# Loading the second dense block of x from GpSimd's queue, and zeroing two x buffers later

## The chip, the cores and the metric

The kernel runs on one core of a Trainium2 chip. A core has TensorE (PE, with its weight loads as PEld), VectorE (DVE), ScalarE (ACT), GpSimd (POOL) and SyncE (SP), which work each through a list of its own and wait for one another on semaphores; transfers run on 16 DMA engines that all queues share. The metric is the device time of one execution in microseconds (us), taken as the median of several.

## What is computed

A causal depthwise convolution over seven tokens, with softmax weights per head, is followed by a feed-forward layer whose hidden value is the largest of three products. Inputs and outputs are float32.

```python
# x: 8 x 4160 x 192, weight: 8 heads x 7, w1, w2, w3: 192 x 768, w_out: 768 x 192
w = softmax(weight)                                     # per head, over the 7 taps
y[b, s, h, :] = sum_k w[h, k] * x_padded[b, s + k, h, :]  # six zero rows ahead of each sequence
y = y.reshape(33280, 192)
h = maximum(maximum(y @ w1, y @ w2), y @ w3)            # 33280 x 768
out = h @ w_out                                         # 33280 x 192
```

The kernel writes the maximum as w3's product plus a maximum of the differences: it keeps `wd` = w1 - w3, w2 - w3 in fp16, takes `max(relu(y @ (w1 - w3)), y @ (w2 - w3))` as the hidden value, and adds `y @ (w3 @ w_out)` through a small matrix `m`.

## The kernel before, in words

The 33280 tokens are cut into 65 blocks of 512 tokens. Blocks 0 to 3 are "dense": their convolution reads x in pieces of 112 rows (`xf`, float32, five pieces to a block), cast to two zero-padded fp16 tiles `xz[t][0]` and `xz[t][1]`. Blocks from 4 on take another road: x is loaded as rows of 39 partitions at two places of an `xf` buffer (partitions 0 to 38 and 64 to 102), GpSimd casts partitions 0 to 102 in one instruction (L199), and since partitions 39 to 63 hold no rows there, partitions 32 to 63 of such a buffer are zeroed once (`zero_x`, L140 on ACT, L137 elsewhere) before its first load of this kind. There are seven `xf` buffers; blocks 4, 5 and 6 use buffers 4, 5 and 6 for the first time and then share them in turn.

The order on each engine is written out by hand. The list of SP's queue at the start is: x0 (two transfers, L167), the first third of the weights (columns 0 to 255) as three transfers of 128 rows (L229) and three of 64 rows (L233), x1 (one transfer of 112 x 5 pieces of 768 bytes, 420 KB, L167), the second third by L229, the other two thirds of the 64-row parts by L233, the last third by L229, w_out (`wos`, L248), x2, x3, and, once their buffers are zeroed, x4, x5, x6.

While these come in, the start of the compute lists is:

- DVE zeroes tiles, casts x0 to `xz[0]` (L216), copies a part of the convolution's band (L297), makes the differences `wd` (L312), zeroes one half of buffer 6 (L137), casts one half of block 0's convolution (L393), moves the lower rows of w3 up by 64 partitions (L316), makes one more difference.
- ACT zeroes buffer 4 (L140), copies its part of the band, zeroes all of buffer 5 (L140), casts the other half of block 0's convolution (L393), zeroes the other half of buffer 6 (L140), casts its share of x1 (L216).
- POOL makes an identity matrix, waits for x1, casts its share of it to `xz[1]` (L216), then casts w3 (L320), moves the rest of w3 up (L316), makes four differences (L312), casts again, copies across (L323), casts w_out to `wo` (L713) and casts x2 and x3 to `xz` (L216).
- PE keeps itself warm, makes the band (L293), does the convolution of block 0 (L388, output D), the first products of block 0 that need only `wd` columns 0 to 255 and one half of the convolution (L541, part "F"), the convolution of block 1 (L388), the other products of blocks 0 and 1 in turn (L541), transposes w3 (L338), multiplies the hidden values of block 0 by `wo` (L613), does the convolution of block 2 (L388), makes `m` (L347), and from block 2 on runs a steady loop: products of one block (L517) between the output products of the block before (L582) and convolutions of later blocks (L367).

Of the kernel before, what the change touches and what calls it, by code (L numbers as in the profile page):

```python
# [15 lines left out]
P = 128  # L16
# [7 lines left out]
HALF = P // 2  # L24
# [4 lines left out]
def kernel(  # L29
# [12 lines left out]
    nc = tc.nc  # L42
    ctx.enter_context(tc.manual_schedule())

    B, SEQ, D = x.shape
# [12 lines left out]
    for b in range(B):  # L58
        s = nfull * NBLK
        while s < SEQ:  # L60
            n = min(SEQ - s, NBLK - off)
# [28 lines left out]
    NR = NBLK // TOK // 2  # L90
# [3 lines left out]
    def rows_of(t):  # L94
        rows = [(b, S + o) for (b, S, N, off) in blocks[t] for o in range(0, N, TOK)]
        assert len(rows) == 2 * NR
        return rows
# [23 lines left out]
    def get_x(t):  # L121

        if not 0 <= t < NB or t in xin:
            return
        if t < XBUF:
            xbuf.append(const.tile([P, NR, D], FP32, name=f"xf_{t}"))
        xf = xbuf[t % XBUF if t < NDENSE + XBUF else NDENSE + (t - NDENSE - XBUF) % 3]
        assert all(v[0] is not xf for v in xin.values())
        xin[t] = [xf, 0, ()]

    def zero_x(t, q0=0, q1=NR, eng=None):

        if t >= NDENSE:
            get_x(t)
        xf = xbuf[t]
        if eng is not None:
            eng.memset(xf[TOK:HALF, q0:q1, :], 0.0)  # L137
            return
        zero = idle[TOK:HALF, 0:D]
        nc.scalar.copy(out=xf[TOK:HALF, q0:q1, :],  # L140
                       in_=bass.AP(tensor=zero.tensor, offset=zero.offset,
                                   ap=[list(zero.ap[0]), [0, q1 - q0], [1, D]]))

    def load_x(t, eng=nc.sync):
        if not 0 <= t < NB:
            return
        loaded.add(t)
        get_x(t)
        xf = xin[t][0]
        if t < NDENSE:  # L150
            todo = [(0, c[3], c[1] * SEQ + c[2], i) for i, c in enumerate(chunks_of[t])]
        else:
            todo = [(HALF * (i // NR) + (0 if s else LAP), KR if s else TOK,
                     b * SEQ + s - (LAP if s else 0), i % NR) for i, (b, s) in enumerate(rows_of(t))]
        parts = []
        i, n = 0, len(todo)
        row = [c[2] for c in todo]
        while i < n:
            k = i
            while k + 1 < n and todo[k + 1][:2] == todo[i][:2] and row[k + 1] - row[k] == row[i + 1] - row[i]:  # L160
                k += 1
            step = row[i + 1] - row[i] if k > i else 0
            p0, rlen, _, q0 = todo[i]
            q1 = todo[k][3] + 1
            src = bass.AP(tensor=x.tensor, offset=row[i] * D,
                          ap=[[D, rlen], [step * D, q1 - q0], [1, D]])
            eng.dma_start(out=xf[p0:p0 + rlen, q0:q1, :], in_=src)  # L167
            if parts and parts[-1][0] == rlen:
                parts[-1] = (rlen, parts[-1][1], q1)
            else:  # L170
                parts.append((rlen, q0, q1))
            i = k + 1
        xin[t] = [xf, todo[0][0], parts]
# [33 lines left out]
    def cast_dense(t, copies, slots_=range(CYC // 32)):  # L207
        xf, _, parts = xin.pop(t)
        for v, copy in enumerate(copies):
            if copy is None:  # L210
                continue
            for s in slots_:
                cut = GRP * (32 * s // GRP + 1)
                a, b = (32 * s, cut) if v == 0 else (cut, 32 * s + 32)
                for (rl, q0, q1) in parts:
                    copy(  # L216
                        out=xz[t][v][0:rl, q0:q1, :].rearrange("p q (k c) -> p q k c", c=CYC)[:, :, :, a:b],
                        in_=xf[0:rl, q0:q1, :].rearrange("p q (k c) -> p q k c", c=CYC)[:, :, :, a:b])
# [8 lines left out]
    def load_wa(f):  # L227
        for st, n, wsrc in ((w3s, 0, moe_w3), (ws, 0, moe_w1), (ws, 1, moe_w2)):
            nc.sync.dma_start(out=st[:, n, f], in_=wsrc[0:P, f])  # L229

    def load_wb(f):
        for st, lo, n, wsrc in ((w3s, 0, 1, moe_w3), (ws, 0, 2, moe_w1), (ws, HALF, 2, moe_w2)):
            nc.sync.dma_start(out=st[lo:lo + HALF, n, f], in_=wsrc[P:D, f])  # L233

    wk = const.tile([NHEAD, SMALL], FP32, name="wk")[:, 0:KW]
    nc.scalar.dma_start(out=wk[:], in_=weight)
# [4 lines left out]
    load_x(0)  # L241
    load_wa(slice(0, PW))
    load_wb(slice(0, PW))
    load_x(1)
    load_wa(slice(PW, 2 * PW))
    load_wb(slice(PW, DFF))
    load_wa(slice(2 * PW, DFF))
    nc.sync.dma_start(out=wos[:], in_=moe_w_out.rearrange("(j p) c -> p j c", p=P))  # L248
# [3 lines left out]
    make_identity(nc, ident[:])  # L252
    ident16 = const.tile([P, P], FP16)
    nc.gpsimd.tensor_copy(out=ident16[:], in_=ident[:])
    idle = const.tile([P, NBLK], FP16)
    nc.vector.memset(idle[:], 0.0)
    def keep_warm(widths, pool, tag):

        ps = pool.tile([P, NBLK], FP32, tag=tag, name="idle")
        for n in widths:  # L260
            nc.tensor.matmul(ps[:, 0:n], lhsT=idle[:, 0:P], rhs=idle[:, 0:n], start=True, stop=True)
# [27 lines left out]
    for lo, hi, copy in ((0, CUT, nc.scalar.copy), (CUT, WIN, nc.vector.tensor_copy)):  # L289
# [6 lines left out]
        for a in range(4):  # L296
            copy(out=band[32 * a:32 * a + 32, :, 32 * a + lo:32 * a + hi],  # L297
                 in_=bps[:, 0:hi - lo, :].rearrange("p c h -> p h c"))
    zero_x(5)
    keep_warm((NBLK,) * 3, psp, "p")  # L300


# [7 lines left out]
    def make_wd(n, j0, j1, eng=nc.vector):  # L310
        f = slice(P * j0, P * j1)
        eng.tensor_sub(out=wd[:, n, f], in0=ws[:, n, f], in1=w3s[:, n // 2, f])  # L312

    def copy_w3(copy, j0, j1):
        f = slice(P * j0, P * j1)
        copy(out=w3s[HALF:P, 1, f], in_=w3s[0:HALF, 1, f])  # L316

    def cast_w3(j0, j1):
        f = slice(P * j0, P * j1)
        nc.gpsimd.tensor_copy(out=w3h[:, :, f], in_=w3s[:, :, f])  # L320
# [8 lines left out]
    def w_of(i, c, j):  # L329
        n = side(i, c)  # L330
        n = i if n == 0 else NC if n == 1 else 2
        return wd[HALF * i:HALF * (i + 1), n, P * j:P * (j + 1)]
# [110 lines left out]
    def y_all(t, i, c):  # L443
        if t < NDENSE:
            return dense[t][HALF * i:HALF * (i + 1), side(i, c), :]
        a = y_row(t, i)
        s0, s1, s2, s3 = (spot(t, i, c, r) for r in range(4))
        assert s3 - s2 == s1 - s0
        return bass.AP(tensor=a.tensor, offset=a.offset + P * s0,
                       ap=[list(a.ap[0]), [P * (s2 - s0), 2], [P * (s1 - s0), 2], [1, P]])  # L450
# [39 lines left out]
    def meet():  # L490

        emit(True)
        assert not ops
        clock[0] = clock[1] = 0
# [32 lines left out]
    def l1_dense(tiles, parts="FH"):  # L527

        meet()
        for part in parts:  # L530
            order = [(i, v) for i in range(2) for v in tiles] if part == "F" else [(i, v) for v in tiles for i in range(2)]
            for i, (t, j, pools) in order:
                pool, tag = pools[i]
                if (t, j, i) not in open_ps:
                    open_ps[t, j, i] = pool.tile([P, NBLK], FP32, tag=tag, name=f"l{tag}{i}_{t}_{j}")
                    begun.discard((t, j, i))
                if part == "F":
                    a, b = wd[:, i, P * j:P * (j + 1)], dense[t][:, 0, :]
                else:
                    a, b = w_of(i, NC - 1, j), y_all(t, i, NC - 1)  # L540
                nc.tensor.matmul(open_ps[t, j, i][:], lhsT=a, rhs=b,  # L541
                                 start=(t, j, i) not in begun, stop=(t, j, i) in begun)
                begun.add((t, j, i))
# [143 lines left out]
    PQ = ((psp, "p"), (psq, "q"))  # L687
    WW = ((psw, "w"), (psw, "w"))
    WPWQ = ((psw, "w"), (psp, "p"), (psw, "w"), (psq, "q"))
    ACT, DVE = nc.scalar.copy, nc.vector.tensor_copy  # L690
    GP = nc.gpsimd.tensor_copy
    make_wd(0, 0, 2)
    make_wd(1, 0, 2)
    zero_x(6, 4, NR, nc.vector)
    conv_dense(0, (ACT, DVE))
    zero_x(6, 0, 4)
    for t in range(NDENSE, XBUF):
        load_x(t)
    copy_w3(DVE, 0, 2)
    make_wd(2, 0, 2)  # L700
    cast_dense(1, (GP, ACT), (1, 2, 0))
    l1_dense([(0, 0, PQ), (0, 1, PQ)], "F")
    cast_w3(0, 2)
    copy_w3(GP, 2, 6)
    make_wd(2, 2, 4, nc.gpsimd)
# [144 lines left out]
```

## Time and profile before

| what | us |
|---|---|
| median of three runs (lowest, highest) | 452.57 (452.45, 454.37) |
| the profiled execution, its own time | 453.55 |
| its span, first to last instruction | 451.8 |
| PE busy in the span | 445.6 |
| ACT, DVE, POOL busy | 320.4, 356.3, 203.7 |
| granted TensorE clock, mean | 1.000 |
| PE's share of the chain that ended last | 95% |

The span is shorter than the execution's time by 1.75 us, which lies before the first and behind the last instruction. A profile shows one execution; it gives when each instruction ran, what an engine waited for, and in time order the chain of work that ended last. PE is busy for nearly the whole span, so what is left to gain or lose lies where PE is not busy: 7.50 us of the first 10 us are, 9.78 of the next ten, 9.46 of the ten behind those, and 9.97 of those from 30 to 40.

### The profile page before, as it was taken

What the parts mean: (1) busy time and instruction counts of PE and PEld (TensorE: products, weight loads), DVE (VectorE), ACT (ScalarE), POOL (GpSimd) and SP (SyncE); (2) the same over time, 40 slices, a digit from 0 to 9 for tenths busy, and PEclk for the clock granted to TensorE, in tenths of its full rate; (3) what the DMA queues carried; (4) which work ended last, traced back from release to release, by engine and by line L of the source; (5) the groups of instructions that cost most, each with busy time, mean ns of one, the idle gap of its engine ahead of it and who ended that gap; (6) DMA issues with size and microseconds to landing.
All of it is one profiled execution on the core that took longest, in us unless ns stands there. A gap on an engine that the chain in (4) does not pass through costs nothing.

```text
span 451.8 us, 18261 instructions
## 1 busy us (share of the span) xinstructions
PE 445.6 (99%) x7576; PEld 409.5 (91%) x7576; DVE 356.3 (79%) x610; ACT 320.4 (71%) x600; POOL 203.7 (45%) x234
## 2 busy tenths in 40 slices
PE   7999999999999999999999999999999999999997
PEld 4479999999999999999999999999999999999996
DVE  7768778878878787787787887887887887887775
ACT  7867777767777676676776776776776776776664
POOL 2784826556455524724824625526533544224000
DMA  6979999595875659649559749659549677142123
GB/s 201 247 178 160 199 186 209 152 222 160 181 210 149 174 124 210 164 117 204 162 130 196 182 111 199 180 99 227 158 113 197 171 158 143 54 136 75 58 71 106
DMA packets 128242, 72.01 MB, mean 159 GB/s; under 512 B 52320, under 2 KB 127967, under 8 KB 128159
## 3 DMA queue, kind: packets, MB, share of 16 engines
q1 hardware_dynamic: 127999, 70.75, 68.3%
q8 instruction: 59, 0.97, 1.1%
q14 instruction: 24, 0.20, 0.2%
q10 hardware_dynamic: 160, 0.10, 0.1%
HBM read 33.28 MB, written 25.56 MB: 130 GB/s over the span
## 4 chain that ended last, share of the span: by engine, by line
PE 95%; SPq 2%; DMA 2%; POOL 0%; issue 0%; DVE 0%; POOLq 0%
PE po L582 36%; PE lq L517 32%; PE lp L517 22%; PE G L367 3%; DMA wos<-in_moe_w_out_dram 2%; SPq L229 1%; SPq L233 1%; PE po L613 0%; PE D L388 0%; PE po L640 0%; SPq L167 0%; POOL wo L713 0%; PE pm L347 0%; PE po L657 0%; PE po L621 0%
## 5 line engine op out<-in xcount | busy, mean ns | idle before, releaser
L582 PE MATMUL po<-wo,h 64*128 64x192 f16 x3024 | 331.7, 243 | 0.0
L505 DVE TENSOR_TENSOR h<-r,lq 128x512 f16<-128x512 f16 x384 | 262.8, 685 | 84.9 <-ACT r L500 74.9
L500 ACT ACTIVATE r<-lp 128x512 f16<-128x512 f32 x384 | 228.9, 597 | 113.7 <-PE lp L517 102.8
L517 PE MATMUL lp<-yp,wd 64*128 64x512 f16 x1098 | 295.6, 376 | 0.0
L517 PE MATMUL lq<-yp,wd 64*128 64x512 f16 x1098 | 295.5, 376 | 0.0
L582 PEld LDWEIGHTS <-h 64*128 64x128 f16 x3024 | 242.7, 94 | 5.3 <-issue 4.1
L517 PEld LDWEIGHTS <-wd 64*128 64x128 f16 x2268 | 181.7, 94 | 14.8 <-issue 0.2
L199 POOL CAST x<-xf 103x768 f16<-103x768 f32 x122 | 97.1, 824 | 113.8 <-DMA xf<-in_x_dram 109.2
L582 PE MATMUL po<-m,yp 64*128 64x192 f16 x720 | 140.3, 243 | 0.0
L430 POOL COPY yp<-yp 64x1536 f16<-64x1536 f16 (+1 forms) x70 | 90.9, 1298 | 85.1 <-DMA yp<-ys 42.0
L590 DVE TENSOR_TENSOR o<-a,po 128x384 f32<-128x384 f32 x126 | 69.0, 547 | 0.0
L582 PEld LDWEIGHTS <-yp 64*128 64x128 f16 x720 | 66.3, 94 | 0.1
L589 ACT COPY a<-po 128x384 f32<-128x384 f32 x126 | 59.6, 473 | 0.0
L407 ACT CAST ys<-G 128x480 f16<-128x480 f32 (+1 forms) x53 | 25.4, 530 | 9.5 <-PE G L367 9.5
L407 DVE CAST ys<-G 128x480 f16<-128x480 f32 (+1 forms) x53 | 30.1, 610 | 0.0
L367 PE MATMUL G<-x,band 39*32 39x240 f16 (+3 forms) x1024 | 16.5, 242 | 0.0
L367 PEld LDWEIGHTS <-band 39*32 39x32 f16 x1024 | 10.2, 92 | 4.6 <-issue 4.5
L517 PE MATMUL lq<-yd,wd 64*128 64x512 f16 x36 | 9.7, 376 | 0.0
L517 PE MATMUL lp<-yd,wd 64*128 64x512 f16 x36 | 9.7, 376 | 0.0
L541 PEld LDWEIGHTS <-wd 128*128 128x128 f16 (+1 forms) x48 | 3.1, 96 | 6.1 <-issue 2.7
L216 POOL CAST xz<-xf 112x160 f16<-112x160 f32 (+2 forms) x15 | 4.2, 323 | 8.4 <-DMA xf<-in_x_dram 8.3
L388 PEld LDWEIGHTS <-xz 112*32 112x32 f16 x320 | 4.1, 100 | 2.6 <-POOL xz L216 1.1
(79 smaller groups left out, 98.7 us busy)
## 6 DMA issues: line engine op xcount, KB each, us to landing
xf<-in_x_dram SPq DMA_DIRECT2D x113, 234.0 KB
out_dram<-o SPq DMA_DIRECT2D x62, 384.0 KB
wall<-in_moe_w_dram SPq DMA_DIRECT2D x12, 128.0 KB
xf<-in_x_dram SPq DMA_DIRECT2D x7, 204.8 KB
xf<-in_x_dram SPq DMA_DIRECT2D x3, 420.0 KB
yp<-ys SPq DMA_TRANSPOSE x70
out_dram<-o SPq DMA_DIRECT2D x5, 192.0 KB
wos<-in_moe_w_out_dram SPq DMA_DIRECT2D x1, 576.0 KB
```

The lines of the kernel that those rows point to most:

```text
L199: nc.gpsimd.tensor_copy(out=x16s[t0][0:K, :, :, u, r, :].rearrange("p h j c -> p j h c"), in_=xf[0:K, 4 * r:4 * r + 4, :].rearrange("p j ( ...
L229: nc.sync.dma_start(out=st[:, n, f], in_=wsrc[0:P, f])
L233: nc.sync.dma_start(out=st[lo:lo + HALF, n, f], in_=wsrc[P:D, f])
L367: nc.tensor.matmul(G[2 * (k // per) + i][TOK * j:TOK * (j + 1), k % per, :], lhsT=band[row, h, HALF * i + LAP:HALF * i + KR], rhs=x16s[t0] ...
L407: copy(out=slots[t][:, i % 2, :, :, GRP * h0:GRP * (h0 + per)].rearrange("p u r (h c) -> p h (u r) c", c=GRP), in_=G[i][:].rearrange("p h ...
L430: nc.gpsimd.tensor_copy(out=yp[HALF * i:HALF * (i + 1), 1, :, :, :, :].rearrange("p i u k n -> p (i u k n)"), in_=yp[HALF * (1 - i):HALF * ...
L500: nc.scalar.activation(out=r[:], in_=ps[0][:], func=AF.Relu)
L505: nc.vector.tensor_max(out=hs[t][:, j, :], in0=r[:], in1=q[:])
L517: nc.tensor.matmul(ps[i][:], lhsT=w_of(i, c, j), rhs=y_all(t, i, c), start=(n == 0), stop=(n == NC - 1))
L582: nc.tensor.matmul(ps[b0, i][:, s % 2, :], lhsT=a, rhs=b, start=first, stop=last)
L589: nc.scalar.copy(out=a[:], in_=ps[s - 1, 0][:])
L590: nc.vector.tensor_add(out=outs[t][:, s - 1:s + 1, :], in0=a[:], in1=ps[s - 1, 1][:])
```

## The change

x1 is no longer in SP's queue: the buffer is only reserved there, and the load is issued by GpSimd, right behind its copy of the identity matrix. Everything behind x1 on SP's queue moves up by one place. The move of the first third of w3's lower rows (`copy_w3(…, 0, 2)`) goes from DVE to GpSimd, ahead of GpSimd's share of x1's casts. Buffer 5 is zeroed half by ACT, half by DVE, behind the casts of block 0's convolution and of x1, instead of all by ACT ahead of them. Buffer 6 is zeroed all by GpSimd, behind its share of x1's casts, instead of half by DVE and half by ACT. `load_wb` gets a parameter that keeps its old value in every call.

```diff
-    def load_wb(f):
+    def load_wb(f, eng=nc.sync):
         for st, lo, n, wsrc in ((w3s, 0, 1, moe_w3), (ws, 0, 2, moe_w1), (ws, HALF, 2, moe_w2)):
-            nc.sync.dma_start(out=st[lo:lo + HALF, n, f], in_=wsrc[P:D, f])
+            eng.dma_start(out=st[lo:lo + HALF, n, f], in_=wsrc[P:D, f])
@@
     load_x(0)
     load_wa(slice(0, PW))
     load_wb(slice(0, PW))
-    load_x(1)
+    get_x(1)
     load_wa(slice(PW, 2 * PW))
@@
     nc.gpsimd.tensor_copy(out=ident16[:], in_=ident[:])
+    load_x(1, nc.gpsimd)
     idle = const.tile([P, NBLK], FP16)
@@
-    zero_x(5)
+    get_x(5)
     keep_warm((NBLK,) * 3, psp, "p")
@@
     make_wd(0, 0, 2)
     make_wd(1, 0, 2)
-    zero_x(6, 4, NR, nc.vector)
+    copy_w3(GP, 0, 2)
     conv_dense(0, (ACT, DVE))
-    zero_x(6, 0, 4)
+    make_wd(2, 0, 2)
+    cast_dense(1, (GP, ACT), (1, 2, 0))
+    zero_x(5, 0, 4)
+    zero_x(5, 4, NR, nc.vector)
+    l1_dense([(0, 0, PQ), (0, 1, PQ)], "F")
+    zero_x(6, eng=nc.gpsimd)
     for t in range(NDENSE, XBUF):
         load_x(t)
-    copy_w3(DVE, 0, 2)
-    make_wd(2, 0, 2)
-    cast_dense(1, (GP, ACT), (1, 2, 0))
-    l1_dense([(0, 0, PQ), (0, 1, PQ)], "F")
     cast_w3(0, 2)
     copy_w3(GP, 2, 6)
```

## The prediction

> **What bounds the kernel now.** I read the page's busy times first, then the chain that ended last, in order of time, then PE's own waits, and last the timeline and the transfers of the first microseconds, where the change is. The busy times, and the waits of PE over the whole span (us in total, times, longest):
>
> ```profile
> PE 445.6 (99%) x7576; PEld 409.5 (91%) x7576; DVE 356.3 (79%) x610; ACT 320.4 (71%) x600; POOL 203.7 (45%) x234
> ...
> PE lp L541 <- ACT yd L393: 0.7, 1, 0.7
> PE D L388 <- POOL xz L216: 0.6, 1, 0.6
> PE po L613 <- POOL wo L713: 0.5, 1, 0.5
> PE lq L541 <- DVE h L505: 0.2, 1, 0.2
> ```
>
> PE bounds all but the start. Asked for the waits of PE behind 25 us, the trace lists none. So whatever moves PE's entry into its steady loop moves the end by as much, and nothing else that the change touches can. The four waits are all that the start can give, beside a start of the whole chain that is earlier. That chain (start, us, what):
>
> ```profile
> 5.05 0.59 SPq L167
> ...
> 8.98 1.42 SPq L229
> ...
> 11.40 7.90 DMA wos<-in_moe_w_out_dram
> 19.42 1.15 POOL wo L713
> 20.61 2.14 PE po L613 x24
> 22.75 1.04 PE D L388 x76
> ```
>
> SP's queue sends the loads one behind the other; the nineteenth transfer on it, w_out, lands at 19.30; POOL casts it; PE waits 0.54 us for the cast. The timeline shows the other gate, x1 (start, us, instructions, idle time before them and what ended it):
>
> ```profile
> 6.11 1.48 ACT L140 CAST xf<-idle 32x1536 f32<-32x1536 f16 x1
> 7.61 0.58 ACT L393 CAST yd<-D 128x512 f16<-128x512 f32 x1
> 8.24 0.59 PE L541 MATMUL lp<-yd,wd 128*128 128x512 f16 x2 [0.65 <-ACT yd L393]
> 9.45 0.91 POOL L216 CAST xz<-xf 112x160 f16<-112x160 f32 x3 [7.79 <-DMA xf<-in_x_dram]
> 9.88 1.30 PE L388 MATMUL D<-band,xz 112*32 112x103 f16 x80 [0.61 <-POOL xz L216]
> 21.06 3.39 POOL L216 CAST xz<-xf 112x240 f16<-112x240 f32 x12 [0.50 <-DMA xf<-in_x_dram]
> ```
>
> x1 is issued at 5.05 and its readers start at 9.40 (ACT) and 9.45 (POOL): 4.35 us. And ACT's zeroing of buffer 5 stands in front of the cast that PE waits for at 8.24. The transfers from 0 to 16 us, in slices of 0.4 us:
>
> ```profile
> GB/s 0 0 0 0 29 188 334 349 295 159 141 328 287 156 174 113 58 100 338 361 373 308 336 305 353 205 195 159 228 256 215 247 224 161 276 326 321 315 326 325
> ```
>
> From 5.2 to 7.2 us the engines moved 156, 174, 113, 58 and 100, 120 GB/s on average, against some 330 where they are busy: 0.42 MB of room, about what x1 needs (112 x 5 x 768 bytes, 0.43 MB).
>
> **The change, step by step.**
>
> *Zeroing of buffer 5 off ACT.* The 1.48 us at 6.11 goes from ahead of ACT's cast at 7.61. How early can that cast be? In block 1's convolution the first half is done 0.89 us behind PE's start (9.88; ACT's cast starts at 10.77, having waited for PE). Block 0's starts at 6.26, so its cast can start at 7.14, ends at 7.73, and PE's part F starts at 7.78 instead of 8.24: 0.46 us. DVE's other half isn't needed before part H.
>
> *PE to x1's convolution.* F's four matmuls took PE from 8.24 to 9.27 (its wait before 9.88 is 0.61), so 1.03 us; from 7.78 they end at 8.81. If xz is cast by then, convolution 1 starts at 8.81 instead of 9.88: 1.07 us.
>
> *x1 from GpSimd.* POOL is free at 1.67 (its cast at L254 starts at 1.38 and takes 0.29) and idle until 9.45. The trace has no transfer issued by POOL, so what it takes to write 560 row pieces is bounded from both sides. From below by nothing. From above by GpSimd's rate on data: 0.82 us for 768 elements of a row at L199, 1.07 ns each; at eight words a piece, 4480 words, 4.8 us. The nearest row is SP's issue of the same load, 0.59 us; I take twice that, 1.2 us. To landing I take the slow 4.35 us of SP's x1: 1.67 + 1.2 + 4.35 = 7.2 us (6.0 to 10.8 by the bounds). POOL first moves w3's rows, for which it needs a transfer issued at 3.15; by the same 4.35 us that lands by 7.50, the move (half of the 0.61 us that L316 takes for twice the columns) ends at 7.83, the first cast (0.38) at 8.21: 0.6 us ahead of 8.81. So x1 may land as late as 8.4 at no cost, and brings nothing from 9.4 on. ACT's share of the casts comes behind 7.73 and costs nothing either.
> A sentence from a page: the Trainium skill, "DMA: Bandwidth & Descriptors", section "Anatomy of one DMA — SWDGE (gpsimd) path", gives 2.0 us plus bytes over 436 GB/s; by it, as an estimate, x1 would land at 1.67 + 2.0 + 1.0 = 4.7 us; no run here shows it yet.
>
> *What x1 now shares the engines with.* x0 and the first weights. x0's casts start at 4.62 behind DVE's own zeroing, the differences L312 at 6.47 behind the band copies, so neither waits for its data now. All of x1 put ahead of the last of them costs 1.3 us (0.43 MB at 330 GB/s); F needs its second difference by 8.2 (two matmuls behind 7.78). The issues at 1.69 to 2.68 and 4.35 us give 7.0 at worst, plus 0.42 for the difference: covered.
>
> *Zeroing moved behind.* ACT's half of buffer 5 (0.83 us) comes behind its casts of x1, 7.83 to 8.61, and ends at 9.44, ahead of its next cast at 9.70. DVE's half (0.70) comes behind its cast (7.62 to 8.31) and the difference (0.43): 8.74 to 9.44, and its next cast can start at 10.17 (11.24 less 1.07). Buffer 6 on POOL: 0.10 us for one element, 0.20 for 128 in the rows of its memsets, so 0.8 ns each, and 1.3 us for 1536. POOL: moves to 7.83, casts 0.91, zeroing 1.3, cast of w3 0.61: 10.7. Its next copy waits for weights that came at 12.15 before, and for some 10.9 now. Covered, narrowly; without that cover up to 0.3 us more, which POOL's 1.70 us of idle time before `wo` takes up. The loads of x5 and x6 are issued from 17 us on: no wait.
>
> *SP's queue.* One issue fewer: 0.64 us (5.05 to 5.69) for all behind it. x1's bytes are out of the way: 1.3 us. The 1.42 us at 8.98, where an issue of usually 0.43 took a microsecond longer with seven transfers in front, can go too: at most 0.64 + 1.42 = 2.06. I take 1.3 us for the landing of w_out and x2, between 0.64 and 2.06.
>
> *Sum.* PE would be ready for L613 0.54 + 1.07 = 1.61 us earlier; `wo` is ready 1.3 us earlier; the later counts: 1.3. Block 2's convolution waits for POOL's casts of x2, whose data come 1.3 us earlier: the same. The profiled execution took 453.55 (span 451.8 and 1.75 around it) and would take 452.25. Its time is 0.98 above the median, 452.57, so I put the gain on the median: 451.3. From the bounds of the landing: 0.64 to 1.61, 451.0 to 451.9.
>
> **The rivals.**
>
> *A. w_out lands no earlier.* Its 7.90 us are far more than 576 KB need (1.8 us at 330 GB/s), so something else holds its last part back; if that has its own time, POOL's cast stays at 19.42 and the 0.54 us of PE grow to 1.61. Gain 0 to 0.3: 452.4. Against it: what holds it may come with PE's progress, and move.
>
> *B. More is gained.* If the second stretch tightens too: DVE's difference at 12.18 took 0.85 us where others took 0.42, and PE waited 0.22 at 14.28; both gone and w_out 2.06 earlier gives 1.61 + 0.43 + 0.22 = 2.3: 450.3. Against: three things must go right at once.
>
> *C. GpSimd's writing is held up by DVE; slower.* DVE is busy from 0.80 to 7.24 with hardly a gap. If POOL gets its turn only at 7.24, x1 lands at 7.24 + 1.2 + 4.35 = 12.8, its casts start 3.4 us later than now, and PE loses that less its 0.54 us of waiting at L613: 2.9, 455.4. It decides from a landing at 9.9 on. If only the six casts at 4.62 (0.92 us) hold it up, x1 lands at 8.1 and nothing is lost; at the upper bound of the writing, 10.8, it is 0.9 us, 453.5. Most of DVE's work there is zeroing, which reads nothing; that speaks against the full price.
> The Trainium skill, "SBUF — State Buffer", section "SBUF: two separate sides", warns of this: while DVE runs in a two-port mode GpSimd can't write descriptors, so a transfer from its queue appears blocked. By its section "Who interferes with whom", an instruction with at most one SBUF input outside those modes doesn't contend. By that, memsets would leave POOL free, the small price would hold, and this trace, without a transfer of POOL's, can't say.
>
> That the change doesn't do what it says is no rival of weight: in the order of instructions POOL's load stands right behind L254 and waits for no semaphore.
>
> **How the numbers follow.** Forecast (gain 0.6 to 1.6) 0.52; A 0.13; B 0.14; C 0.21. About 0.5% (2.3 us, 450.3 and 454.8) can be told from no change. Faster by more: B's further half and the forecast's scatter from run to run, 0.14. Slower by more: C at its full price, 0.17. Within: 0.69. The forecast's own range is 450.6 to 452.2; with A, most of B and C's small price, 450.0 to 454.0 holds 8 in 10.
>
> **What would show it.** The casts of x1 starting on POOL at 6 to 8.2 and convolution 1 at about 8.8 show the first step; ACT's cast of block 0 at 7.1 the zeroing; w_out's issue ahead of 10.8 and POOL's `wo` at about 18.1 the queue; L613 at about 19.3 the sum. If `wo` stays at 19.4, A is right; if convolution 1 starts behind 9.9 with POOL or ACT waiting for x1, C. A wait of PE behind 25 us would make the whole reckoning wrong.

## The result, and the profile after

The kernel after takes 454.96 us in the median (453.94 to 456.33, 20 runs), the kernel before 453.32 (452.45 to 456.06, 20 runs) beside it: a ratio of 1.0030, 95% interval 1.0017 to 1.0043. By this ratio it is slower by 1.4 us (0.8 to 1.9), where 451.3 was forecast; the two medians differ by 1.64. Its profiled execution took 455.40, span 453.6.

The waits of PE over the whole span of the kernel after (us in total, times, longest):

```profile
PE lp L542 <- DVE wd L313: 2.3, 1, 2.3
PE idle L262 <- DVE idle L257: 1.2, 1, 1.2
PE lq L542 <- DVE h L506: 0.2, 1, 0.2
```

The three waits that were to go are gone (ACT's cast, POOL's `xz`, POOL's `wo`). One has come in their place: PE waits 2.3 us for the weight differences that DVE makes. (The diff adds a line ahead of these: L313 here is L312 of the kernel before, L542 is L541, L614 is L613, L389 is L388.) The same place in order of time (start, us, instructions, idle time before them and what ended it):

```profile
1.62 0.94 POOL L167 DMA_DIRECT2D xf<-in_x_dram  x1
...
6.95 0.59 ACT L394 CAST yd<-D 128x512 f16<-128x512 f32 x1 [0.86 <-PE D L389]
8.94 0.78 ACT L216 CAST xz<-xf 112x160 f16<-112x160 f32 x3 [1.41 <-DMA xf<-in_x_dram]
9.12 2.39 SPq L233 DMA_DIRECT2D wall<-in_moe_w_dram  x3
9.19 0.76 DVE L313 TENSOR_TENSOR wd<-wall 128x256 f16<-128x256 f32 x2 [2.75 <-DMA wall<-in_moe_w_dram]
...
9.68 1.03 PE L542 MATMUL lp<-yd,wd 128*128 128x512 f16 x2 [2.33 <-DVE wd L313]
...
11.49 1.71 PE L389 MATMUL D<-band,xz 112*32 112x103 f16 x80
```

Read it upwards. PE's first products start at 9.68 instead of 8.24; DVE's difference starts at 9.19, having waited 2.75 us for a transfer of weights; in the kernel before it started at 6.47. ACT's cast at 6.95 is where the prediction wanted it, and has nobody to serve. x1, the load that was brought forward, is cast at 8.94 instead of 9.40. So a load that PE needs second came earlier, and the one that it needs first came later.

The landing of a transfer is the last of the sixteen increments that its DMA engines write to its semaphore. By these, w1's first third (issued at 2.21) landed at 9.10 instead of 5.42, w2's (issued at 2.69) at 9.45 instead of 5.80, and x1 (issued at 1.62) at 8.87 instead of 9.33. Transfers from 2 to 10 us by queue (packets, MB, share of the 16 engines' time), and x1's load among those issued there (size, us to landing):

```profile
q1 hardware_dynamic: 1647, 1.38, 66.3%
q0 software_dynamic: 112, 0.43, 23.8%
...
xf<-in_x_dram POOLq DMA_DIRECT2D x1, 420.0 KB, 7.2
```

x1 took 7.2 us from issue to landing, on a queue of its own. Its 0.43 MB went in 96 packets with data, 80 of 4608 bytes (six rows of 768), while each packet of SP's queue is one row of 768, 1024 or 2048 bytes. From 4.0 to 5.5 us, 41 packets of x1's queue with data (39 of them of 4608 bytes) and 30 of SP's were moved: turns of about one and one, in which x1 got some six times the bytes (39 x 4608 against 30 x 1024). In the second profile of the kernel after it was 72 and 78. The Trainium skill, "DMA: Bandwidth & Descriptors", section "Queues, rings and completion order", says that each DMA engine goes round the queues that have work, a whole packet at a time; the count of turns in this stretch agrees. It gives 9 to 17 descriptors as a typical packet; here SP's packets were of one row and most of x1's of six, so a turn of x1 moved 4608 bytes and one of SP's 1024.

Windows of the kernel after (busy us and count of PE, PEld, DVE, ACT, POOL; then granted clock, DMA share, GB/s):

```profile
4.00:5.00 1.00, 1.00 (x37) 0.96 (x34) 0.95 (x5) 0.85 (x2) 0.00 (x0) 1.00 0.69 125
5.00:6.00 1.00, 1.00 (x3) 0.15 (x1) 0.97 (x7) 0.96 (x4) 0.00 (x0) 1.00 0.78 240
...
8.00:9.00 1.00, 0.00 (x0) 0.00 (x0) 0.00 (x0) 0.06 (x1) 0.00 (x0) 1.00 1.06 257
9.00:10.00 1.00, 0.33 (x1) 0.13 (x2) 0.81 (x3) 0.98 (x4) 0.18 (x1) 0.71 0.47 136
10.00:11.00 1.00, 1.00 (x4) 0.30 (x2) 0.89 (x2) 0.57 (x1) 0.94 (x4) 0.50 0.52 150
11.00:12.00 1.00, 1.00 (x30) 0.51 (x31) 0.70 (x1) 0.00 (x0) 0.94 (x3) 0.50 0.53 137
```

Two things are to be seen. From 4 to 5 us, with two queues at work, the engines moved 125 GB/s, less than the 253 of the kernel before. And behind PE's empty microsecond (8 to 9) the granted clock falls to 0.50, by the trace's clock record from 9.42 to 12.83: the products of part F take 1.03 and 1.06 us instead of 0.59 and 0.59, x1's convolution 1.71 instead of 1.30. The Trainium skill, "TensorE: Matmul & The Clock Gate", section "What's actually happening", lists two states, half and full clock, half after an idle window of some 3.4 us; the rows agree with the two steps (0.71 is a mean over a slice), but PE's wait here was 2.33 us, and was enough.

PE comes to w_out's products (L614) at 22.13 instead of 20.61, and from there the shift nearly stays: 1.72 at 43.5 us, 1.72 at 396.7, 1.86 at the end.

### The profile page after: what moved, and what is told of

Same layout as the page of the kernel before. It is cut to its first block, busy times and chain, and to the rows that moved or that the text cites. A ratio compares the mean times of both kernels' runs of the same rounds, so it can differ in the third digit from the quotient of the medians.

```text
span 453.6 us, 18264 instructions
## 1 busy us (share of the span) xinstructions
PE 446.7 (98%) x7576; PEld 409.3 (90%) x7576; DVE 356.8 (79%) x609; ACT 319.0 (70%) x599; POOL 207.6 (46%) x237
## 4 chain that ended last, share of the span: by engine, by line
PE 97%; DMA 2%; DVE 1%; SPq 0%; issue 0%; DVEq 0%
PE po L583 36%; PE lq L518 31%; PE lp L518 22%; PE G L368 3%; DMA wall<-in_moe_w_dram 2%; PE D L389 1%; PE lp L542 1%; PE lw L542 1%; PE po L641 0%; PE po L614 0%; PE lq L542 0%; DVE wd L313 0%; DVE h L506 0%; PE pm L348 0%; SPq L167 0%
## 5 line engine op out<-in xcount | busy, mean ns | idle before, releaser
L542 PEld LDWEIGHTS <-wd 128*128 128x128 f16 (+1 forms) x48 | 3.1, 99 | 8.5 <-issue 3.4
L389 PEld LDWEIGHTS <-xz 112*32 112x32 f16 x320 | 4.4, 106 | 2.2 <-POOL xz L216 0.8
L542 PE MATMUL lp<-yd,wd 128*128 128x512 f16 (+1 forms) x12 | 4.0, 420 | 2.3 <-DVE wd L313 2.3
```

The source lines that it names most:

```text
L389: nc.tensor.matmul(ps[32 * g:32 * g + 32, lo:hi], lhsT=xz[t][v][0:rlen, q, 32 * s:32 * s + 32], rhs=band[0:rlen, h, cc:cc + hi - lo], star ...
L542: nc.tensor.matmul(open_ps[t, j, i][:], lhsT=a, rhs=b, start=(t, j, i) not in begun, stop=(t, j, i) in begun)
```

## The experiments

Each kernel ran in five rounds beside the kernel before, whose median was 453.35 us in the first four, and 453.24, 453.07 and 453.51 in the next groups of four. All times of landing are last increments, all starts those of the profiled execution. The head below is the first 20 us, up to w_out's products (L613 or L614, L615 where an edit adds a line).

**Each half alone.** zero_only is the kernel after with x1 back on SP's queue:

```diff
-    get_x(1)
+    load_x(1)
...
-    load_x(1, nc.gpsimd)
```

> Only the zeroing and the move of w3's rows are changed; x1 stays on SP's queue. Theory (the loss is the load of x1 on GpSimd's queue, which holds back the first weights): no loss; part F starts at about 7.8 us instead of 8.24, convolution 1 still waits for x1 and starts at about 9.9, time within 0.7 us of before (ratio 0.998 to 1.001). Rival (the moved zeroing delays something): about 1.6 us slower than before, ratio 1.003 or more.

Measured: 453.36, ratio 1.0008 (0.9993 to 1.0024). PE's rows from 7 to 30 us:

```profile
7.80 0.59 PE L541 MATMUL lp<-yd,wd 128*128 128x512 f16 x2 [0.25 <-ACT yd L393]
...
9.51 1.29 PE L388 MATMUL D<-band,xz 112*32 112x103 f16 x80 [0.69 <-POOL xz L216]
...
19.60 2.14 PE L613 MATMUL po<-wo,h 128*128 128x192 f16 x24
...
26.63 0.96 PE L388 MATMUL D<-band,xz 112*32 112x103 f16 x65
27.89 0.36 PE L388 MATMUL D<-band,xz 112*32 112x103 f16 x15 [0.29 <-issue]
```

The head does what the prediction worked out for this half: 7.80 for the first products (7.78 was forecast), L613 a whole microsecond earlier (19.60 against 20.61). But the end is only 0.16 earlier. Most of what is gained at 19.6 is lost before 30, part of it inside convolution 3, which stops after 65 of its 80 matmuls for "issue". More of this below.

load_only is the kernel before with x1 on GpSimd and the zeroing where it was.

```diff
-    load_x(1)
+    get_x(1)
...
+    load_x(1, nc.gpsimd)
```

> Only the load of x1 is moved to GpSimd's queue, in the kernel before. Theory: all of the loss, part F at about 9.7 us, granted clock 0.5 behind PE's wait, 1.2 to 2 us slower than before (ratio 1.003 to 1.0045). Rival (the moved zeroing does it): part F at 8.3 at the latest, ratio at most 1.000.

Measured: 454.63, ratio 1.0027 (1.0011 to 1.0044). PE's waits up to 30 us:

```profile
PE lp L542 <- DVE wd L313: 2.3, 2, 1.6
```

w1 and w2 land at 8.77 and 9.10, the first products start at 9.35. The load is what costs; the zeroing is not to blame.

**Which queue.** act_queue sends x1 at 2.37 on ACT's queue instead, in packets of one row like SP's (buffer 4's zeroing goes to GpSimd for it):

```diff
-    load_x(1, nc.gpsimd)
...
+    load_x(1, nc.scalar)
...
-    zero_x(4)
+    zero_x(4, eng=nc.gpsimd)
```

> The changed kernel with x1 issued by ScalarE at 3.1 us, on its hardware queue, so that its packets run in the same stretch (about 4 us on) and in the same quantity as from GpSimd's queue; GpSimd zeroes buffer 4 in ScalarE's place. Theory (it is the software queue's large packets, 4608 bytes, that take turns one for one with the weights' 1024 bytes): x1's packets are single rows of 768 bytes, the weights get their share, part F by 8.1 us, convolution 1 at about 8.9, 0.5 to 1.3 us faster than before (ratio 0.997 to 0.999). Rival (any early x1 takes the transfers' time from the weights, whatever the queue): part F at 9 us or later, a wait of PE for DVE's difference of over 1.2 us, ratio 1.002 or more.

Measured: 454.59, ratio 1.0036 (1.0018 to 1.0053). w1's third now lands at 6.88, but w2's at 8.55; the first pair of products starts at 7.59, the second waits 0.88 us for DVE and starts at 9.05. So a second queue with packets of single rows is already enough to hold w2 up. Long packets may make it worse (w1 at 9.10 with them), but x1 was issued ahead of w1 there and behind it here, and no run separates the two. L614 is at 20.54 in the profile, no later than before, but this execution, the slowest of its twelve, then lost 3.07 us to "issue" in convolution 3.

sp_first sends the same early bytes on SP's own queue, right behind x0 and ahead of every weight:

```diff
     load_x(0)
+    load_x(1)
     load_wa(slice(0, PW))
     load_wb(slice(0, PW))
-    get_x(1)
...
-    load_x(1, nc.gpsimd)
```

> The kernel after with x1's load back on SP's queue, but as the second issue, right behind x0 and ahead of every weight; the zeroing stays moved. The same early bytes as in the kernel after, now as single rows on the queue that also carries the weights. Theory (early bytes ahead of the weights cost, whatever the queue): w1's first third lands 1.3 us or more later than in the kernel before (5.42), its issue being 0.64 later and x1's 0.43 MB in front of it, so F starts at 8.5 to 9.5 and the end is 0.3 to 1.6 us later than before: 453.7 to 455.0. Rival (only the software queue's long packets harm the weights): w1 lands by 6.7, F starts by 8.2, convolution 1 by 9.2, the end 0 to 1 us earlier: 452.4 to 453.4.

Measured: 453.46, ratio 0.9999 (0.9984 to 1.0013). Windows as above:

```profile
4.00:5.00 1.00, 1.00 (x37) 0.96 (x34) 0.95 (x5) 0.84 (x2) 0.00 (x0) 1.00 0.96 312
5.00:6.00 1.00, 0.82 (x3) 0.10 (x1) 0.97 (x7) 0.96 (x4) 0.00 (x0) 1.00 1.10 302
6.00:7.00 1.00, 0.78 (x68) 0.78 (x72) 0.40 (x2) 0.15 (x2) 0.00 (x0) 1.00 1.03 289
```

DVE's differences, each waiting for its weights:

```profile
7.17 0.43 DVE L312 TENSOR_TENSOR wd<-wall 128x256 f16<-128x256 f32 x1 [0.74 <-DMA wall<-in_moe_w_dram]
7.83 0.43 DVE L312 TENSOR_TENSOR wd<-wall 128x256 f16<-128x256 f32 x1 [0.24 <-DMA wall<-in_moe_w_dram]
```

This is the decisive run. All of x1 lies ahead of the weights here too, on one queue, and they come 1.65 and 2.0 us later: w1 at 7.08 instead of 5.42, w2 at 7.81 instead of 5.80. Their issues are 0.54 later behind x1's; the other 1.1 and 1.5 lie around the 1.3 us that the prediction had taken for x1's bytes. It is covered: the first products start at 7.65, the second pair at 8.32 with hardly a wait. The engines move 312, 302 and 289 GB/s from 4 to 7 us where they moved 125, 240 and 270 in the kernel after. My theory of this run (early bytes harm on any queue) had the delay of w1 right and its effect wrong: the first products did not come at 8.5 or later, and the time is that of the kernel before. The rival's w1 by 6.7 was not met either. The same bytes harm on a second queue.

sp_mid puts x1 on SP's queue between the 128-row and the 64-row thirds:

```diff
     load_wa(slice(0, PW))
+    load_x(1)
     load_wb(slice(0, PW))
-    get_x(1)
...
-    load_x(1, nc.gpsimd)
```

> The kernel after with x1 on SP's queue, behind the 128-row thirds of the weights and ahead of their 64-row thirds. Theory (what counts is which bytes stand ahead of the first products): the 128-row thirds land as before (by 5.5), the 64-row ones 1 to 2 us later (7 to 8), F starts at 7.6 to 8.6, x1 lands by 7.5 and convolution 1 starts at 9 to 9.5; L613 no later than in the kernel before (20.61), the end 0 to 1 us earlier: 452.4 to 453.4. Rival (any transfer of x1 ahead of 5 us costs a microsecond, as load_only and act_queue do): 454.3 to 454.9.

Measured: 453.83, ratio 1.0015 (1.0001 to 1.0029). w1 and w2 land at 6.17 and 7.00, the first products start at 7.63, but the 64-row thirds land at 9.3 to 9.9, and PE waits 1.66 us for `xz` and starts convolution 1 at 10.31. That is neither the theory (452.4 to 453.4) nor the rival (454.3 or more): by the medians not as bad as a second queue, worse than sp_first.

**When.** pool_late leaves x1 on GpSimd, behind its own zeroing of buffers 5 and 6, pool_mid behind that of buffer 5 alone (the memsets on the other engines are left out for those):

```diff
+    get_x(4)
+    zero_x(5, eng=nc.gpsimd)
+    zero_x(6, eng=nc.gpsimd)
     load_x(1, nc.gpsimd)
```

> The kernel after with x1 still on GpSimd's queue, but behind GpSimd's zeroing of buffers 5 and 6, so that its first packets come at about 6 us instead of 3.76, when the first thirds have landed. Theory (the harm is in the time at which x1 shares the engines with the first weights): the first thirds land as in the kernel before (4.4 to 6.0), F starts at 7.6 to 8.0 without a wait for DVE, x1 lands by 8 to 9.5, convolution 1 starts at 9.5 to 10.5, the end is within 0.5 us of the kernel before: 452.9 to 453.9. Rival (a software transfer costs by itself, whenever it comes, as it holds up the second thirds of the weights and w_out as well): the end 1 us or more later, 454.3 or more.

> The kernel after with x1's issue on GpSimd behind the zeroing of buffer 5 alone (now on GpSimd), so at about 3.0 us, between the kernel after (1.62) and pool_late (4.38). Theory (the harm is that x1 is sent on a second queue while the first weights are under way on SP's): something of it, x1 landing at 6.5 to 8.5, w2's first third at 5.8 to 8.5, F between 8.0 and 9.3, the median between pool_late's and after's: 453.3 to 454.6. Rival (only a start ahead of the weights harms, as in after): F by 8.0, 452.9 to 453.3.

Measured: pool_late 453.07, ratio 0.9991 (0.9979 to 1.0002); pool_mid 453.01, ratio 0.9992 (0.9979 to 1.0006). GpSimd's rows in pool_late (start, us):

```profile
1.74 2.69 POOL L137 MEMSET xf<- 32x1536 f32 x2
4.38 0.94 POOL L167 DMA_DIRECT2D xf<-in_x_dram  x1
...
8.91 0.85 POOL L216 CAST xz<-xf 112x160 f16<-112x160 f32 x3 [2.15 <-DMA xf<-in_x_dram]
```

The same software queue, the same packets, issued 2.76 us later: w1 and w2 land at 5.63 and 6.12, x1 still at 8.75, ahead of the kernel before, and the loss is gone. With the issue at 3.06 (pool_mid) they land at 5.69 and 6.19 and the loss is gone too. The first products of pool_late start at 8.87 all the same, later than its theory had them, but not for the weights: beside GpSimd's zeroing, DVE's small multiply for the band (L288, L284 before) took 0.98 us instead of 0.22, the band came later, and convolution 0 and the first products ran at about half pace (1.91 us for 1.11, 1.03 for 0.59). The trace of pool_late has no clock record; pool_late_x6, with the same head, has its first one, of full clock, at 9.92, where twelve other profiles have theirs at 4.4 to 7.6. The software queue is not costly by itself; what counts is what is under way when it starts. Both lie at the lower edge of the kernel before without being told from it.

**How much.** dose2 sends two of x1's five pieces at once from GpSimd and three from SP where x1 was:

```diff
+    load_x(1, own=(2, NR))
...
-    load_x(1, nc.gpsimd)
+    load_x(1, nc.gpsimd, (0, 2))
```

> The kernel after with two of x1's five pieces on GpSimd at once and the other three on SP's queue where the kernel before has x1. Theory (the harm grows with the bytes that come early on the second queue): the first thirds of the weights some 0.4 of the 3.65 us late that all five cost, w2 by 7.3, F by 8.6, the median 453.4 to 454.3. Rival (a second queue costs as such, whatever it carries): F at 9.2 or later, 454.5 or more.

Measured: 453.32, ratio 1.0002 (0.9988 to 1.0017). w1 and w2 at 6.39 and 6.89, and PE's first products:

```profile
7.59 0.59 PE L543 MATMUL lp<-yd,wd 128*128 128x512 f16 x2 [0.25 <-ACT yd L395]
```

No wait for DVE. Here w2 lands at 6.89, in sp_first at 7.81, and both are covered; the harm begins behind that. Its profiled execution ended the earliest of all (L615 at 19.75, end 0.8 earlier than before); its median did not follow.

**The clock.** keep_warm is the kernel after with nine products of zeros behind convolution 0, whose results nobody reads:

```diff
     conv_dense(0, (ACT, DVE))
+    keep_warm((NBLK,) * 9, psp, "p")
```

> The changed kernel with nine more idle products of 512 columns (1.9 us) on TensorE behind block 0's convolution, where it waited 2.3 us. Theory (two terms: the weights late by 1.4 us at part F, and a granted clock of 0.5 from 9.6 to 12.5 us behind the wait, worth 1.2 us): part F still at 9.7, granted clock 1.0 throughout, convolution 1 at 10.7 instead of 11.5, products of block 0 by the output weights (L614 in the changed kernel) about 1 us earlier than 22.1, time 0.7 to 1.2 us below the changed kernel, about 453.9 or ratio 1.0005 to 1.0015 against before. Rival (the clock costs nothing, other engines set the pace behind part F): as the changed kernel, ratio 1.003.

> keep_warm once more, for a second profile: its median was 1.3 us above before, and its profiled run's head no later than before's (L614 at 20.56, 29.6 us checkpoint at -0.05). Theory (the head varies, and the first profile was one of its luckier runs): the wait for weights in front of F is longer, L614 at 21 or later, 454.4 to 455 in the median. Rival (the head is as in the first profile, and the runs lose it later, to PE's instructions): L614 by 20.7 and a wait for issue between 22 and 45 us.

Measured: 454.64, ratio 1.0028 (1.0012 to 1.0044), and again 454.75, ratio 1.0025 (1.0013 to 1.0036). The granted clock is 1.00 (0.999 at least) in all 24 executions, and L614 comes at 20.56 and 20.83, 1.3 to 1.6 us earlier than in the first profile of the kernel after. Of this, 0.4 us are there when the first products start (9.26 and 9.23 against 9.68); the other 0.9 to 1.1 go with the low clock. In the medians it counts for little: 0.2 to 0.3 us against the first group of the kernel after, under 0.2 against the second, by the ratios 0.1 to 0.5. The theory's 453.9 was not reached.

> The kernel after once more, for a second profile of it. Theory (early x1 holds back the first weights, and the wait lets the granted clock fall): F starts at 9.3 to 9.9 again behind a wait for DVE of 1.7 to 2.5 us, a granted clock of 0.5 to 0.8 in the 3 us behind it, L613 at 21 to 22.3; 454.6 to 455.4 in the median. Rival (the first profile was an odd one): F by 8.5, the clock at 1.0 throughout, L613 by 20.6.

> load_only once more, for a second profile: its median was 1.2 us above before, its profiled run's L614 at 20.64 and end at +0.26. Theory (the head varies): F at 9.3 or later again, the granted clock below 1.0 behind it, L614 at 21 or later; 454.2 to 454.9 in the median. Rival (lost later, to PE's instructions): L614 by 20.7 and a wait for issue between 22 and 45 us.

after_again: 454.79, ratio 1.0037 (1.0020 to 1.0053); F at 9.44 behind 2.10 us of waiting, the clock at 0.50 from about 11.2 to 14.6, L614 at 21.68. It is as the theory had it, and the first profile was no odd one. Over both groups of the kernel after, the 19 executions with a mean clock of 0.996 or less lie at 455.3 and the 13 others at 454.3 to 454.45. The executions with a low clock are slower by some 0.9 us, and the others are still a microsecond above the kernel before. The 0.9 is not shown to be the clock's: the clock may fall just where the weights come latest, and keep_warm, without a low clock in any execution, lies above the 13. load_only_2: 454.69, ratio 1.0030 (1.0012 to 1.0048), L614 at 20.75, no wait for issue behind 22 us. Of its profile neither side was met: the head is only 0.14 late, and nothing is lost behind it. In the profiled executions of load_only and keep_warm (453.8 to 454.2) some 0.5 to 0.9 us of their medians' excess does not show.

**The later loss.** In sp_first PE came to L613 at 19.62, and the end was 0.46 later than before. Its rows:

```profile
19.62 2.14 PE L613 MATMUL po<-wo,h 128*128 128x192 f16 x24 [0.25 <-POOL wo L714]
...
26.58 0.96 PE L388 MATMUL D<-band,xz 112*32 112x103 f16 x65
28.59 0.36 PE L388 MATMUL D<-band,xz 112*32 112x103 f16 x15 [1.06 <-issue]
```

Transfers from 22.6 to 26.0 us in sp_first, by queue:

```profile
q1 hardware_dynamic: 933, 0.69, 79.8%
q14 instruction: 1, 0.01, 0.7%
```

and in pool_late, which lost nothing there:

```profile
q1 hardware_dynamic: 271, 0.19, 18.9%
q8 instruction: 1, 0.02, 1.8%
```

Queue q8 moves 59 packets of 16384 bytes in an execution of the kernel after, and PE's matmuls and weight loads are 2 x 7576 = 15152: 257 to a packet, 64 bytes each. No other engine has nearly as many, so I take them as PE's next instructions. The packet that was wanted in convolution 3 came at 23.43 in pool_late, at 24.92 in the kernel before, at 25.19 in zero_only, 26.08 in sp_first and 28.80 in act_queue. In pool_late the loads of x2 to x6 had thinned out by then (0.19 MB in these 3.4 us); in sp_first they went on (0.69 MB), and no packet came among them. That the loads hold the packet back is argued from this and not shown: in dose2 it came at 23.34 with the transfers still at 251 GB/s. In the last three of the list PE went on 1.3 to 1.5 us behind the packet's end, having waited 0.29, 1.06 and 3.07. The Trainium skill, "Runtime: NRT & Kernel Launch", section "Terms", says that an engine's instructions are refilled in blocks of 16 KiB, which agrees.

To get the head's gain through, four kernels load x6 behind x7, at some 25 us instead of 20:

```diff
-    for t in range(NDENSE, XBUF):
+    for t in range(NDENSE, XBUF - 1):
         load_x(t)
...
     load_x(7)
+    load_x(6)
```

> sp_first with the load of x6 moved on SP's queue from ahead of 20 us to behind the load of x7, some 25 us. In sp_first PE came to w_out's products (L613) 1.0 us earlier than in the kernel before, and lost 1.4 us inside convolutions 2 and 3 to its next instructions, whose 16 KB packet came only at 26.08 us, when the loads of x thinned out. Theory (the loads of x4 to x6 hold that packet back, and so the head's gain is lost): the packet comes by 24.5, no wait for issue in convolution 3, the loop from 29.6 us on and the end 0.7 to 1.2 us earlier than before: 452.0 to 452.6 in the median. Rival (the packet comes at a time of its own): the packet still at 25.5 or later, the wait stays, 453.2 to 453.6.

> pool_late with the same move of x6's load. There the packet came at 23.43 and nothing was lost in convolution 3, so theory: the same profile of the head, the end within 0.3 of pool_late's, 452.8 to 453.1, with fewer runs above 453.3. Rival: x6's load, being later, meets the loads of x7 and x8 and costs a wait of PE behind 29 us: 453.5 or more.

> The kernel before with the same move of x6's load alone: the control. Its profiled run lost nothing in convolution 3 (the packet came at 24.92), so the profile should keep its end within 0.2 us; if part of its 35 runs lose up to a microsecond there (452.2 to 455.4), the median falls by 0.2 to 0.5, to 452.8 to 453.1. Rival (x6's load plays no part): the median within 0.1.

> The kernel after with the same move of x6's load. Its profiles lose nothing in convolution 3 (packets at 26.66 and 25.91, PE later by as much). Theory (the loss of after is all in the head: weights late, then a low clock): 454.3 to 455.0, L614 still 1 us or more later than 20.6. Rival (a part of it is the packet's wait in the runs that were not profiled): 453.8 or less.

Measured: sp_first_x6 456.19, ratio 1.0046 (1.0026 to 1.0065); pool_late_x6 453.97, 1.0030 (1.0010 to 1.0050); before_x6 455.60, 1.0050 (1.0029 to 1.0072); after_x6 456.95, 1.0078 (1.0046 to 1.0109), of 9, 12, 9 and 7 executions. All four are slower than the kernel before, and of the four theories' times none was met; the rival of pool_late_x6 was. PE's longest waits in sp_first_x6 behind 18 us:

```profile
PE po L582 <- issue: 4.9, 2, 2.5
```

The theory was right on its packet (24.20 instead of 26.08, no wait in convolution 3) and wrong on the sum. x6's load met those of x7 and x8, the next packets came at 32.74 and 39.82 (29.70 and 33.98 in sp_first), and PE waited for them twice, 4.9 us in all. The profile of pool_late_x6 shows such a wait too (2.12 us at 34.48), and that of after_x6 (1.39 at 35.61). So moving the load moved the wait. Not so in before_x6: its profiled execution lost 3 us ahead of 29 us without a wait for "issue". There DVE's copy of `yd` (L399) took 2.97 us from 25.44, where the kernel before needs 0.29, while GpSimd cast x from 25.11 to 28.26, and PE waited 1.90 us for it. The head of sp_first_x6 was also 0.8 us later than sp_first's (first products at 8.49 against 7.65, w1 at 7.92 against 7.08), without an edit there: so much a head varies.

All kernels without the x6 edit, in order of w2's landing (us):

```
kernel        x1 from            w1     w2     first products  L613/L614  median   ratio
zero_only     SP, as before      5.24   5.73   7.80            19.60      453.36   1.0008
before        SP, as before      5.42   5.80   8.24            20.61      453.32   1
pool_late     GpSimd at 4.38     5.63   6.12   8.87            19.78      453.07   0.9991
pool_mid      GpSimd at 3.06     5.69   6.19   8.28            20.24      453.01   0.9992
dose2         2/5 GpSimd, 1.62   6.39   6.89   7.59            19.75      453.32   1.0002
sp_mid        SP, fourth load    6.17   7.00   7.63            20.75      453.83   1.0015
sp_first      SP, behind x0      7.08   7.81   7.65            19.62      453.46   0.9999
keep_warm_2   GpSimd at 1.62     8.15   8.45   9.23            20.83      454.75   1.0025
load_only_2   GpSimd at 1.62     8.21   8.51   8.79            20.75      454.69   1.0030
act_queue     ACT at 2.37        6.88   8.55   7.59            20.54      454.59   1.0036
after_again   GpSimd at 1.62     8.86   9.04   9.44            21.68      454.79   1.0037
load_only     GpSimd at 1.62     8.77   9.10   9.35            20.64      454.63   1.0027
keep_warm     GpSimd at 1.62     8.68   9.15   9.26            20.56      454.64   1.0028
after         GpSimd at 1.62     9.10   9.45   9.68            22.13      454.96   1.0030
```

The line falls between 7.8 and 8.4 us: every kernel whose w2 lands by 7.81 has a ratio of at most 1.0015, every other one of at least 1.0025. The landings are those of one execution each, and the intervals of the ratios nearest to the line overlap (sp_mid up to 1.0029, keep_warm_2 from 1.0013).

## Why the prediction was wrong, step by step

*The step that failed is "What x1 now shares the engines with".* It took x1 as 0.43 MB put ahead of the weights, 1.3 us at 330 GB/s, had the first weights land by "7.0 at worst", and called that covered. Its price is about right for one queue: sp_first measured 1.1 and 1.5 us beside the later issue. With x1 issued by GpSimd at 1.62 they came 2.7 to 3.7 us later (w1 at 8.15 to 9.10 against 5.42), in the kernel after at 9.10 and 9.45, and PE waited 2.33 us for them. The traces show two things there: the engines took turns by packets of 4608 against 1024 bytes, and in seven of eight profiles they moved less while both queues were at work. How much each of them takes isn't separated; act_queue, with rows of 768 bytes, held w2 up by 2.75 us too. The step had the right limit: it wanted the second difference by 8.2, 0.42 of it DVE's, and in sp_first a w2 at 7.81 is covered.

*The "0.42 MB of room"* at 5.2 to 7.2 us, part of the same reckoning, was room that sp_first filled from SP's own queue (302 and 289 GB/s from 5 to 7 us, where there were 181 and 78). The kernel after filled much of it too (240 and 270), but lost ahead of it, from 4 to 5 us (125 where there were 253). A gap in the transfers tells that nothing was moved, not that another queue could move it at the same price.

*Zeroing of buffer 5 off ACT* was right: the cast starts at 6.95 (forecast 7.14), and the first products, where the weights are there, at 7.80 (forecast 7.78). *x1 from GpSimd* was near in the issue (0.94 us, 1.2 taken) and short in the landing: 8.87 for 7.2, inside the bounds of 6.0 to 10.8; the estimate of 4.7 beside it was further off. *PE to x1's convolution* at 8.81 was reached by nobody; sp_first came nearest, with its bulk at 9.40. *Zeroing moved behind* cost nothing, as forecast.

*SP's queue* went the other way. An issue of the second thirds had to wait for w1's late landing (the one at 9.12 above, 2.5 us late), a long issue like that of 1.42 us was still there (1.23 at 10.27), and w_out was issued at 13.14 instead of 11.40: 1.74 later, not 1.3 earlier. In pool_late it was 0.21 earlier.

*Sum*: "whatever moves PE's entry into its steady loop moves the end by as much" held to 0.2 us over 350 us, from 44 us on, in every profile. But w_out's products are not that entry. Between them and 30 us lies PE's instruction packet, and it has, as an estimate, some 0.4 us of slack in the kernel before (it ended at 26.26, PE could go on from 27.8 by the 1.5 us above, and came to the place at 28.2): zero_only and sp_first came to L613 a microsecond earlier and ended 0.16 earlier and 0.46 later. dose2 and pool_late, whose packet came earlier (23.34 and 23.43), kept 0.78 of 0.86 us and 0.38 of 0.84. So a good part of the 1.3 us might have been lost there even if x1 had cost nothing; no kernel's median is below the one before by more than the noise. That the trace of before lists no wait behind 25 us was true, and says nothing of one just out of sight. The base was low as well: 452.57 was the median of three runs, 453.32 that of twenty.

*The rivals.* C named the right sign and, with 455.4, the time of the profiled execution, but by luck: its mechanism didn't happen. GpSimd's load was issued at once (1.62 to 2.56) while DVE was busy; the page of the Trainium skill that stood beside it, "SBUF — State Buffer", section "SBUF: two separate sides", warns of a hold-up that this load did not meet. A was right that `wo` comes no earlier (its cast starts at 20.11, 19.42 before), and it did not matter. B's further gains were not seen.

What stays open is how the 1.4 us of the median divide. The low clock hits 19 of 32 executions, and without it (keep_warm) the time falls by 0.5 us at most; the table puts the rest with the late weights. But in the profiled executions of load_only and keep_warm the late weights cost only 0.3 to 0.6 us at the end, against 1.1 to 1.4 in the median. Whether the other executions have later weights still, or lose it to an instruction packet or to a copy of DVE's as in before_x6, two profiles each did not show.

## What to carry to other kernels

A load moved to a second queue does not only come earlier: while both queues have work, it can take turns with the first by packets, and its packets may be longer. Price it by who lands last among the loads that PE needs first, and start it when those are through, or put it in their queue at its place. Before a gain at the head is booked at the end, look for what comes at a time of its own between the two, here PE's next instructions.

## What the runs showed of the hardware

- All of x1 on a second queue moved less than on one: from 4 to 5 us 101 to 135 GB/s in seven of the eight profiles (252 in after_again), against 312 with the same bytes on SP's queue (sp_first) and 315 with two of five pieces on the second (dose2).
- In the profiled executions a wait of PE for the weights of 2.33 us (after), 2.10 (after_again) and 1.76 (after_x6), and one of 3.07 for "issue" (act_queue), was followed by a granted clock of 0.50 for 3.41 us. Waits of 1.56 (load_only) and 1.45 (load_only_2) were not, and neither were longer ones for "issue": 2.12 (pool_late_x6), 2.42 and 2.48 (sp_first_x6). So the length of the wait alone does not decide; what does, the runs do not show.
- PE's instructions come in packets of 16 KB, each of which takes 0.9 to 2.7 us, and PE stood still for 0.3 to 3.1 us in convolution 3 when one came late (zero_only, sp_first, act_queue).
- DVE's copy of 64 x 512 took 2.97 us beside GpSimd's casts (before_x6, 25.44 us), 0.29 in the kernel before.
